# Linear attention into a two-layer MLP on one core: the first batch's preparation dealt out anew between GpSimd, ScalarE and VectorE, its first rows by head pairs, and two load gates moved

## The chip, the cores and the metric

The kernel runs on one core of one Trainium2 chip. The metric is device time in microseconds (us) of one execution; lower is better. The core has five engines that work through their own instruction streams: TensorE (PE; its weight loads are shown as PEld), VectorE (DVE), ScalarE (ACT), GpSimd (POOL) and SyncE (SP), which here only issues DMAs. GpSimd issues DMAs too. Engines wait for each other by semaphores.

## The reference

The computation is a linear attention, whose output is the input of a two-layer MLP with a leaky ReLU:

```
q, k, v: (8 batches, 8 heads, 576 rows, 64)   float32, 0.1 * randn
q_s = exp(q - max over the 64);       q_s /= sum over the 64
k_s = exp(k - max over the 576 rows); k_s /= sum over the 576 rows
kv  = k_s^T v      (64 x 64 for each batch and head)
a   = q_s kv       -> x: (4608 tokens, 512)
h   = x @ w_in     (512 x 2048)
g   = max(0.01 h, h)
out = g @ w_out    (2048 x 512), float32
```

## The kernel before, in words

*Layout.* A batch's q, k or v is one tile of 128 partitions x 4 head slots x 9 rows x 64. A partition holds 9 rows of a head, so 64 partitions are a head and a slot holds two heads, one on each half of the partitions. The name `gg` in the code counts pairs of slots (0 and 1), `hh` the half of the partitions. Column block g = 2 * hh + gg of x is 128 wide; there are four of them, and layer 1 takes them in the order 0, 2, 1, 3 (L451). So blocks 0 and 2 come from pair 0, blocks 1 and 3 from pair 1.

*Tiles of the MLP.* The 4608 tokens are nine tiles of 512. Layer 1 of a tile is 16 units (one per 128 columns of w_in), each followed by the leaky ReLU on ScalarE (`leaky`, L461); layer 2 accumulates over the same 16 blocks of w_out. Tile 0 is cut in two halves of 256 tokens for layer 1, so it has 32 units in pairs and then 16 steps of layer 2. The attention of the later batches is hung between these units: `at(t, u, ...)` (L484) puts functions behind unit u of tile t and `run` calls them, so the order of every engine's instructions is written out by hand; no scheduler moves them. Each engine works strictly in that order.

*Batch 0* has nothing to hide behind: its preparation is written out from L509 to L558. Its q is taken in three parts: rows 0 to 3 (`RA`, enough for the first 256 tokens), rows 4 and 5 (`R1`) and rows 6 to 8 (`R2`). The steps: `q_first` (L228) takes the maxima of q on VectorE and 16 small exps on ScalarE; `k_tree` (L149) takes k's maxima over the 9 rows on VectorE, `k_max_pe`, `k_all_dve` and `k_all_pe` carry them over the partitions with TensorE, `k_sub_ps` (L352) subtracts them on VectorE, `k_exp` (L202) is on ScalarE; `v_cast` (L209) turns v into bf16 for TensorE, on ScalarE for batch 0; `kv_pair` (L360) makes kv of one pair of slots, `kd_rec` and `kd_one` scale it into `kd`; `q_transpose` and `q_keep` turn the normalised q; `attend` (L408) multiplies it with kd and copies the result to xT. `wake` (L322) issues matmuls on a tile of zeros that nothing reads, which keep TensorE busy.

*Queues and gates.* SP issues, in this order, q's rows 0 to 3, the two halves of k, the two halves of v, q's other rows; then a tiny hold (`hold_sync`, L504: a copy of 256 bytes out of w_in, which makes SP wait for that piece of w_in), and behind it k, q and v of batch 1; then a hold on w_out and batch 2. GpSimd issues w_in in two halves of four loads (`load_w_in`, L129; half 0 is columns 0 to 1023, and of each half the first two loads are the column blocks 0 and 2, the last two the blocks 1 and 3), and w_out in five pieces. Ahead of each group stands a copy of one 4-byte element (a dummy, L510, L535, L565) that waits for some load or value, so that the group is not issued earlier.

*PSUM.* Six banks are shared by all short-lived products (`psB_pool`), two hold layer 2's sums. A matmul into a bank waits until the bank's last reader is done.

Tile 0's first four pairs of units take blocks 0 and 2 of all four first, and then, behind the attend of blocks 1 and 3, the rest:

```
for j in range(0, 8, 2):
    ...
    for i in range(2):
        layer1(j + i, ph[:, i], 0, 256, slice(0, 2), i == 0)
    ...
attend(0, [1, 3], 0, 256, nc.scalar)
```

Of the kernel before, what the change touches and what calls it, by code (L numbers as in the profile page):

```python
# [8 lines left out]
FP32 = mybir.dt.float32  # L9
# [11 lines left out]
R = 9  # L21
# [4 lines left out]
def kernel(  # L26
# [60 lines left out]
    R1, R2 = slice(4, 6), slice(6, R)  # L87
# [140 lines left out]
    def q_first(b, rs):  # L228

        n = rs.stop - rs.start  # L230
        nmax = small_pool.tile([P, HL, n], FP32, name="nmax")
        qsum = small_pool.tile([P, n, HL], FP32, name="qsum")
        for hs in (slice(0, 2), slice(2, 4)):
# [3 lines left out]
            for h in range(hs.start, hs.stop):  # L237
                for r in range(n):
                    nc.scalar.activation(
                        out=st[b]["qe"][:, rs.start + r, h],  # L240
                        in_=st[b]["q"][:, h, rs.start + r],
                        func=AF.Exp,
                        bias=nmax[:, h, r : r + 1],
                        accum_out=qsum[:, r, h : h + 1],
                    )
        st[b]["qsum"] = qsum

    def q_first_rec(b, rs):
        n = rs.stop - rs.start
        st[b]["qrec", rs.start] = qrec = small_pool.tile([P, n, HL], FP32, name="qrec")  # L250
        nc.vector.reciprocal(out=qrec, in_=st[b]["qsum"])
# [70 lines left out]
    def wake(n):  # L322
        for i in range(n):
            nc.tensor.matmul(  # L324
                wake_ps, lhsT=zero[:, 0:P], rhs=zero, start=(i == 0), stop=(i == n - 1)
            )
# [183 lines left out]
    nc.gpsimd.tensor_copy(out=gate[:, 0:1], in_=st[0]["k"][:, HL - 1, R - 1, D - 1 : D])  # L510
# [3 lines left out]
    q_first(0, RA)  # L514
    k_tree(0, H0)
# [6 lines left out]
    k_tree(0, H1, slice(1, 4))  # L522
    k_max_pe(0, 1)
# [5 lines left out]
    wake(2)  # L529
    k_sub_ps(0, 0, HB)  # L530
    k_exp(0, slice(1, 2))
    v_cast(nc.scalar, 0, 0)
    v_cast(nc.scalar, 0, 1)
    k_sub_ps(0, 1)
    nc.gpsimd.tensor_copy(out=gate[:, 0:1], in_=st[0]["k"][:, HL - 1, R - 1, D - 1 : D])  # L535
    load_w_in(1)
    k_exp(0, H1)
    q_first_rec(0, RA)
    q_norm(0, RA)
    kv_pair(0, 0)  # L540
    wake(4)
    q_transpose(0, 0, 4)
    kv_pair(0, 1)
    for hh in range(2):
        kd_rec(0, 0, hh)
        kd_one(nc.vector, 0, 0, hh)
    q_keep(nc.scalar, 0, 0, 4, slice(0, 4, 2))
    q_keep(nc.vector, 0, 0, 4, slice(1, 4, 2))
    attend(0, [0, 2], 0, 256, nc.scalar)
    wake(3)  # L550
    kd_rec(0, 1, 0)
    kd_rec(0, 1, 1)
    kd_one(nc.vector, 0, 1, 0)
    kd_one(nc.vector, 0, 1, 1)
    q_max(0, R1)
    q_sub(nc.gpsimd, 0, R1)
    q_max(0, R2)
# [169 lines left out]
```

## Time and profile before

| | |
|---|---|
| Time, median of 3 runs | 294.86 us (294.04 to 294.93) |
| Profiled execution | 294.82 us |
| Its span, first to last instruction | 293.0 us |
| TensorE (PE) busy | 282.1 us, 96% |
| PE weight loads | 139.9 us, 48% |
| VectorE (DVE) busy | 145.6 us, 50% |
| ScalarE (ACT) busy | 150.7 us, 51% |
| GpSimd (POOL) busy | 85.4 us, 29% |
| Chain that ended last | PE 85%, DVE 6%, POOL 2%, ACT 2% |
| DMA | 45.76 MB, mean 156 GB/s |

Times inside the execution are counted from the start of the span. The profiled execution is 1.8 us longer than its span; what lies outside is the same for any version of the program, so differences are taken inside the span. A row of a timeline gives the start, the duration, the engine, the line, the output tile and the inputs; in brackets stand the idle time before it and what ended that.

### The profile page before, as it was taken

What the parts mean: (1) busy time and instruction counts of PE and PEld (TensorE: products, weight loads), DVE (VectorE), ACT (ScalarE), POOL (GpSimd) and SP (SyncE); (2) the same over time, 40 slices, a digit from 0 to 9 for tenths busy, and PEclk for the clock granted to TensorE, in tenths of its full rate; (3) what the DMA queues carried; (4) which work ended last, traced back from release to release, by engine and by line L of the source; (5) the groups of instructions that cost most, each with busy time, mean ns of one, the idle gap of its engine ahead of it and who ended that gap; (6) DMA issues with size and microseconds to landing.
All of it is one profiled execution on the core that took longest, in us unless ns stands there. A gap on an engine that the chain in (4) does not pass through costs nothing.

```text
span 293.0 us, 4282 instructions
## 1 busy us (share of the span) xinstructions
PE 282.1 (96%) x1661; PEld 139.9 (48%) x1661; DVE 145.6 (50%) x240; ACT 150.7 (51%) x272; POOL 85.4 (29%) x61
## 2 busy tenths in 40 slices
PE   8698999999999999999999999999999999999995
PEld 2266845444544455454445544544455444444443
DVE  3946958696592597189367455735440200110011
ACT  4937684678058605951695338532854066007500
POOL 4645190008019307802930292029300000000000
PEclk9989999999999999999999999999999999999999
DMA  7999999496639553774399138933141310131032
GB/s 257 312 216 391 243 181 401 112 287 258 114 76 310 211 116 90 272 266 89 71 309 292 36 72 282 281 74 72 38 81 38 72 36 1 38 72 36 0 72 74
DMA packets 36580, 45.76 MB, mean 156 GB/s; under 512 B 15952, under 2 KB 19280, under 8 KB 36560
## 3 DMA queue, kind: packets, MB, share of 16 engines
q1 hardware_dynamic: 33120, 41.16, 47.9%
q0 software_dynamic: 3280, 4.20, 8.2%
q8 instruction: 13, 0.21, 0.3%
q10 hardware_dynamic: 160, 0.13, 0.1%
q14 instruction: 7, 0.06, 0.1%
HBM read 36.70 MB, written 9.44 MB: 157 GB/s over the span
## 4 chain that ended last, share of the span: by engine, by line
PE 85%; DVE 6%; POOL 2%; ACT 2%; issue 1%; POOLq 0%
PE pout L473 39%; PE ph L452 39%; PE pkv L295 2%; PE po L440 2%; DVE qe L280 1%; DVE qsum L273 1%; POOL k_raw L195 1%; DVE t L162 1%; PE pout L324 1%; PE psum_qt L389 1%; POOL q_raw L256 1%; PE po L412 1%; ACT xT L422 1%; PE pkv L365 1%; ACT qe L264 1%
## 5 line engine op out<-in xcount | busy, mean ns | idle before, releaser
L473 PE MATMUL pout<-w_out_sb,gj 128*128 128x512 bf16 (+2 forms) x592 | 130.4, 373 | 0.0
L452 PE MATMUL ph<-xT,w_in_sb 128*128 128x512 bf16 (+1 forms) x640 | 127.5, 358 | 1.6 <-ACT xT L422 1.6
L461 ACT ACTIVATE gj<-ph 128x512 bf16<-128x512 f32 x144 | 82.3, 604 | 58.1 <-PE ph L452 57.5
L452 PEld LDWEIGHTS <-w_in_sb 128*128 128x128 bf16 x640 | 62.1, 98 | 63.6 <-issue 2.9
L473 PEld LDWEIGHTS <-gj 128*128 128x128 bf16 x592 | 57.0, 98 | 61.8
L467 DVE COPY out_sb<-pout 128x512 f32<-128x512 f32 (+1 forms) x34 | 22.7, 675 | 90.3 <-PE pout L473 84.7
L195 POOL TENSOR_TENSOR k_raw<-k_raw,kall 128x2304 f32<-128x2304 f32 (+1 forms) x6 | 29.1, 4845 | 85.6 <-DVE kall L187 56.9
L256 POOL TENSOR_TENSOR q_raw<-q_raw,qmax 128x2304 f32<-128x2304 f32 (+4 forms) x11 | 31.1, 2836 | 25.8 <-DVE qmax L226 25.8
L273 DVE TENSOR_REDUCE qsum<-qe 128x36 f32<-128x2304 bf16 (+4 forms) x11 | 19.8, 1799 | 37.5 <-ACT qe L264 37.5
L446 ACT CAST xT<-po 128x320 bf16<-128x320 f32 (+1 forms) x48 | 16.8, 402 | 41.2 <-PE po L440 41.2
L203 ACT ACTIVATE ke<-k_raw 128x2304 bf16<-128x2304 f32 (+2 forms) x11 | 17.5, 1595 | 8.9 <-POOL k_raw L195 8.5
L280 DVE TENSOR_TENSOR qe<-qe,qrec 128x2304 bf16<-128x2304 bf16 (+4 forms) x12 | 21.7, 1807 | 0.4
L226 DVE TENSOR_REDUCE qmax<-q_raw 128x36 f32<-128x2304 f32 (+4 forms) x11 | 19.4, 1789 | 0.0
L264 ACT ACTIVATE qe<-q_raw 128x2304 bf16<-128x2304 f32 (+4 forms) x11 | 16.9, 1536 | 0.8 <-POOL q_raw L256 0.8
L215 POOL CAST vb<-v_raw 128x1152 bf16<-128x1152 f32 x12 | 13.4, 1148 | 0.0
L324 PE MATMUL pout<-zero 128*128 128x512 bf16 x27 | 10.5, 536 | 1.3 <-POOL zero L101 1.3
L162 DVE TENSOR_TENSOR t<-k_raw 128x1024 f32<-128x1024 f32 (+1 forms) x10 | 10.1, 1011 | 0.5 <-DMA k_raw<-in_k_dram 0.2
L467 ACT COPY out_sb<-pout 128x512 f32<-128x512 f32 (+1 forms) x3 | 1.7, 550 | 16.2 <-PE pout L473 16.2
L162 DVE TENSOR_TENSOR t<-t 128x256 f32<-128x256 f32 (+2 forms) x20 | 9.6, 478 | 0.6
L440 PE MATMUL po<-qX,kd 128*128 128x320 bf16 (+1 forms) x48 | 9.8, 286 | 0.0
L295 PEld LDWEIGHTS <-ke 64*128 64x128 bf16 x252 | 7.2, 93 | 3.0 <-ACT gj L461 1.7
L313 DVE TENSOR_TENSOR kd<-pkv,krec 64x128 bf16<-64x128 f32 x28 | 8.1, 289 | 0.7
(55 smaller groups left out, 104.2 us busy)
## 6 DMA issues: line engine op xcount, KB each, us to landing
out_dram<-out_sb SPq DMA_DIRECT2D x70, 128.0 KB, 2.4
q_raw<-in_q_dram SPq DMA_DIRECT2D x7, 1152.0 KB, 8.4
v_raw<-in_v_dram SPq DMA_DIRECT2D x7, 1152.0 KB, 11.0
k_raw<-in_k_dram SPq DMA_DIRECT2D x6, 1152.0 KB, 6.0
k_raw<-in_k_dram SPq DMA_DIRECT2D x4, 576.0 KB, 5.8
w_in_sb<-in_moe_w_in_dram POOLq DMA_DIRECT2D x8, 256.0 KB, 6.8
w_out_sb<-in_moe_w_out_dram POOLq DMA_DIRECT2D x3, 512.0 KB, 12.3
v_raw<-in_v_dram SPq DMA_DIRECT2D x2, 576.0 KB, 7.4
```

The lines of the kernel that those rows point to most:

```text
L162: nc.vector.tensor_tensor(out=o, in0=i0, in1=i1, op=ALU.max)
L195: eng.tensor_tensor(out=ks, in0=ks, in1=st[b]["kall"][:, hs].unsqueeze(2).to_broadcast([P, n, R, D]), op=ALU.subtract,)
L203: nc.scalar.activation(out=st[b]["ke"][:, :, hs].rearrange("p r h d -> p h r d"), in_=st[b]["k"][:, hs], func=AF.Exp,)
L226: nc.vector.tensor_reduce(out=m, in_=st[b]["q"][:, :, rs], axis=AX.X, op=ALU.max)
L256: eng.tensor_tensor(out=qs, in0=qs, in1=st[b]["qmax", rs.start].unsqueeze(3).to_broadcast([P, HL, n, D]), op=ALU.subtract,)
L264: nc.scalar.activation(out=st[b]["qe"][:, rs].rearrange("p r h d -> p h r d"), in_=st[b]["q"][:, :, rs], func=AF.Exp,)
L273: nc.vector.reduce_sum(out=qsum, in_=st[b]["qe"][:, rs], axis=AX.X)
L280: nc.vector.tensor_tensor(out=qes, in0=qes, in1=st[b]["qrec", rs.start].unsqueeze(3).to_broadcast([P, n, HL, D]), op=ALU.mult,)
L452: nc.tensor.matmul(ph, lhsT=w_in_sb[:, cb, j * P : (j + 1) * P], rhs=xT[:, cb, c0 : c0 + n], start=(i == 0 and first), stop=(i == NB - 1 a ...
L461: nc.scalar.activation(out=o, in_=ph, func=AF.Prelu, alpha=LEAKY_SLOPE)
L467: copy(out=out_sb, in_=pout)
L473: nc.tensor.matmul(pout, lhsT=g_sb[j // 2][:, j % 2, tsub * P : (tsub + 1) * P], rhs=w_out_sb[:, j, os], start=(j == 0), stop=(j == NF - 1),)
```

## The change

The diff works on batch 0 and on tile 0's units, and moves some functions of batch 1 between units.

- *Casts of v* for batch 0 go from ScalarE to GpSimd (`v_cast(nc.gpsimd, 0, 0)` and `(nc.gpsimd, 0, 1)`), and GpSimd normalises q's first rows, pair 0 between the casts, pair 1 behind them (`q_first_norm`), where VectorE did all of it in one instruction. `q_first` keeps its sums by pairs and `q_first_rec` is called once for each.
- *By pairs.* Rows 0 to 3 of q are transposed (`q_turn_first`) and kept (`q_keep_first`) pair by pair, and x's blocks 0 and 2 are attended one at a time, before the second pair's kv. The first units of layer 1 take block 0, then block 2 (`begin`), with blocks 1 and 3 attended between (`x1`), and finish with blocks 1 and 3 (`end`). The units of columns 8 to 15 are begun in the same way.
- *Late rows* are three pieces now: rows 4 and 5, 6 and 7, 8. Their subtractions on GpSimd stand ahead of w_out's loads, whose issue moves into a function called behind the first unit. Their exps, sums and normalisations, transposes and attends get other units.
- *Dummies.* The first one waits for the first half of k instead of the second; the one ahead of w_in's second half is replaced by one that waits for k's maxima and stands ahead of the casts, and w_in's second half follows the second normalisation. SP's first hold reads block 1 of w_in's second half (its third load) instead of block 0 (its first).
- *Warm-ups.* Four small float32 matmuls on the maxima of q stand behind the first 14 (`wake_on`); of the others, four zeros before q's transposes become three behind them, and two become three behind k's second maxima.
- *Batch 1.* v's casts stand together ahead of its exps, one group of q's transposes and the eight attends move by some units, and every second copy of these goes to VectorE. The stores of tile 0 are written behind the last step's functions instead of ahead of them.

```
-    R1, R2 = slice(4, 6), slice(6, R)
+    R1, R2, R3 = slice(4, 6), slice(6, 8), slice(8, R)
...
+        st[b]["nmax"] = nmax = small_pool.tile([P, HL, n], FP32, name="nmax")
+        for gg in range(2):
+            hs = slice(2 * gg, 2 * gg + 2)
+            st[b]["qsum", gg] = qsum = small_pool.tile([P, n, 2], FP32, name="qsum2")
...
+    def q_first_rec(b, gg):
+        st[b]["qrec2", gg] = qrec = small_pool.tile([P, RA.stop, 2], FP32, name="qrec2")
+        nc.vector.reciprocal(out=qrec, in_=st[b]["qsum", gg])
+
+    def q_first_norm(eng, b, gg):
+        qes = st[b]["qe"][:, RA, 2 * gg : 2 * gg + 2]
+        eng.tensor_tensor(
+            out=qes,
+            in0=qes,
+            in1=st[b]["qrec2", gg].unsqueeze(3).to_broadcast([P, RA.stop, 2, D]),
+            op=ALU.mult,
+        )
+
+    def q_turn_first(b, gg):
+        n = RA.stop
+        ps = psB_pool.tile([P, 2, n, L], BF16, name="psum_q2", tag=BANK_TAG)
+        for r in range(n):
+            nc.tensor.matmul(
+                ps[:, :, r],
+                lhsT=st[b]["qe"][:, r, 2 * gg : 2 * gg + 2].rearrange("p h d -> p (h d)"),
+                rhs=ident,
+                is_transpose=True,
...
+    def q_keep_first(eng, b, gg):
+        o, i = st[b]["qT"][:, gg::2, RA], st[b]["ps2", gg]
...
+    def wake_on(a, n):
+        for i in range(n):
+            nc.tensor.matmul(
+                wake_ps[0:RA.stop, 0:P], lhsT=a[:, HL - 1], rhs=identf, start=True, stop=True
+            )
...
     wake(14)
-    nc.gpsimd.tensor_copy(out=gate[:, 0:1], in_=st[0]["k"][:, HL - 1, R - 1, D - 1 : D])
+    nc.gpsimd.tensor_copy(out=gate[:, 0:1], in_=st[0]["k"][:, 1, R - 1, D - 1 : D])
     load_w_in(0)
     k_begin(0)
     q_begin(0)
     q_first(0, RA)
+    wake_on(st[0]["nmax"], 4)
     k_tree(0, H0)
...
     k_tree(0, H1, slice(1, 4))
+    nc.gpsimd.tensor_copy(out=gate[:, 0:1], in_=st[0]["kmax"][:, HL - 1, D - 1 : D])
+    v_cast(nc.gpsimd, 0, 0)
...
-    wake(2)
+    wake(3)
+    q_first_rec(0, 0)
+    q_first_norm(nc.gpsimd, 0, 0)
+    v_cast(nc.gpsimd, 0, 1)
     k_sub_ps(0, 0, HB)
     k_exp(0, slice(1, 2))
-    v_cast(nc.scalar, 0, 0)
-    v_cast(nc.scalar, 0, 1)
+    q_first_rec(0, 1)
+    q_first_norm(nc.gpsimd, 0, 1)
+    load_w_in(1)
     k_sub_ps(0, 1)
-    nc.gpsimd.tensor_copy(out=gate[:, 0:1], in_=st[0]["k"][:, HL - 1, R - 1, D - 1 : D])
-    load_w_in(1)
     k_exp(0, H1)
-    q_first_rec(0, RA)
-    q_norm(0, RA)
     kv_pair(0, 0)
-    wake(4)
-    q_transpose(0, 0, 4)
-    kv_pair(0, 1)
...
+    q_turn_first(0, 0)
     wake(3)
+    kd_rec(0, 0, 0)
+    kd_one(nc.vector, 0, 0, 0)
+    q_keep_first(nc.vector, 0, 0)
+    kd_rec(0, 0, 1)
+    kd_one(nc.vector, 0, 0, 1)
     q_max(0, R1)
     q_sub(nc.gpsimd, 0, R1)
+    attend(0, [0], 0, 256, nc.scalar)
+    kv_pair(0, 1)
+    attend(0, [2], 0, 256, nc.scalar)
+    q_turn_first(0, 1)
+    q_keep_first(nc.scalar, 0, 1)
+    for hh in range(2):
+        kd_rec(0, 1, hh)
+        kd_one(nc.vector, 0, 1, hh)
     q_max(0, R2)
     q_sub(nc.gpsimd, 0, R2)
 
-    hold_sync(0, w_in_sb[0:1, 0, F - 128 : F])
+    hold_sync(0, w_in_sb[0:1, 1, F - 128 : F])
...
+    def behind_first_units():
+        nc.gpsimd.tensor_copy(out=gate[:, 0:1], in_=st[1]["k"][:, 0, 0, 0:1])
+        for j0, j1 in ((0, 2), (2, 4), (4, 8), (8, 12), (12, 16)):
+            load_w_out(slice(j0, j1))
+        hold_sync(1, w_out_sb[0:1, 11, 0:128])
+        load_all(2)
...
+    at(0, 0, behind_first_units, lambda: q_rest(R1))
+    at(0, 3, lambda: q_rest(R2))
+    at(0, 13, lambda: attend(0, [0, 2], 256, 256, nc.scalar))
+    at(0, 13, lambda: attend(0, [1, 3], 256, 256, nc.vector))
+    at(0, 13, lambda: q_rest(R3))
+    at(0, 17, lambda: q_transpose(0, 8, 1), lambda: q_keep(nc.scalar, 0, 8, 1))
+    at(0, 21, lambda: attend(0, [0, 1, 2, 3], 512, 64, nc.scalar))
...
-    at(0, 29, lambda: k_exp(1, H1))
-    at(0, 31, lambda: v_cast(nc.scalar, 1, 0), lambda: k_exp(1, H0))
+    at(0, 31, lambda: v_cast(nc.scalar, 1, 0), lambda: v_cast(nc.scalar, 1, 1))
     at(0, 33, lambda: q_exp(1, RA), lambda: q_sum(1, RA), lambda: q_norm(1, RA))
-    at(0, 33, lambda: v_cast(nc.scalar, 1, 1), lambda: q_exp(1, RB), lambda: q_sum(1, RB))
+    at(0, 33, lambda: k_exp(1, H1), lambda: k_exp(1, H0), lambda: q_exp(1, RB))
...
-        at(0, 43, lambda r0=r0, n=n: q_transpose(1, r0, n), lambda r0=r0, n=n: q_keep(nc.scalar, 1, r0, n))
+        at(0, 44, lambda r0=r0, n=n: q_transpose(1, r0, n), lambda r0=r0, n=n: q_keep(nc.scalar, 1, r0, n))
     for i in range(8):
-        at(0, (45, 45, 46, 46, 46, 47, 47, 47)[i], lambda i=i: attend(1, [GS[i // 2]], 288 * (i % 2), 288, nc.scalar))
+        at(0, 46 + i // 4, lambda i=i: attend(1, [GS[i // 2]], 288 * (i % 2), 288, (nc.scalar, nc.vector)[i % 2]))
...
+    def begin(js, parts):
+        phs = [psB_pool.tile([P, 2, 256], FP32, name="ph", tag=BANK_TAG) for _ in js]
+        for i, between in parts:
+            for j, ph in zip(js, phs):
+                for h in range(2):
+                    layer1(j + h, ph[:, h], 0, 256, slice(i, i + 1), h == 0, False)
+            for fn in between:
+                fn()
+        return phs
+
+    def end(j, ph, half, part, first):
+        for h in range(2):
+            layer1(j + h, ph[:, h], 256 * half, 256, part, first and h == 0, h == 1)
+            if h == 1:
+                leaky(g_sb[j // 2][:, :, 256 * half : 256 * half + 256], ph)
+            run(0, 16 * half + j + h)
+
+    def x1():
+        attend(0, [1], 0, 256, nc.scalar)
+        attend(0, [3], 0, 256, nc.vector)
+        q_max(0, R3)
+        q_sub(nc.gpsimd, 0, R3)
+
+    t1 = (lambda: q_transpose(0, 4, 2), lambda: q_keep(nc.scalar, 0, 4, 2))
+    t2 = (lambda: q_transpose(0, 6, 2), lambda: q_keep(nc.vector, 0, 6, 2))
+    for j0, parts in ((0, ((0, (x1,)), (1, ()))), (8, ((0, t2), (1, ())))):
+        js = range(j0, j0 + 8, 2)
+        if j0:
+            for fn in t1:
+                fn()
+        for j, ph in zip(js, begin(js, parts)):
+            end(j, ph, 0, slice(2, 4), False)
+    for j in range(0, NF, 2):
+        end(j, psB_pool.tile([P, 2, 256], FP32, name="ph", tag=BANK_TAG), 1, slice(0, 4), True)
...
-        if j == NF - 1:
-            for tsub in range(NTS):
-                store(tsub * P, pout[tsub])
         run(0, 32 + j)
+    for tsub in range(NTS):
+        store(tsub * P, pout[tsub])
```

More of the change, by code (lines that the diff above doesn't have):

```diff
@@ L644 @@
     g_sb = g_tiles()
[L645 to L660 removed]
+    def begin(js, parts):
[8 more added lines that the diff above has]
+    def end(j, ph, half, part, first):
+        for h in range(2):
+            layer1(j + h, ph[:, h], 256 * half, 256, part, first and h == 0, h == 1)
[18 more added lines that the diff above has]
+        end(j, psB_pool.tile([P, 2, 256], FP32, name="ph", tag=BANK_TAG), 1, slice(0, 4), True)
     pout = [psO_pool.tile([P, O], FP32, name="pout") for _ in range(2)]
```

68 lines of the change are left out of this document (17 added, 51 removed).

## The prediction

> **What bounds the kernel now.** I read the page first (TensorE's share, the 40 slices), then the timeline of the first 45 us, the landing of single transfers, and the busy time by stretches of 2 us.
>
> ```profile
> span 293.0 us, 4282 instructions
> PE 282.1 (96%) x1661; PEld 139.9 (48%) x1661; DVE 145.6 (50%) x240; ACT 150.7 (51%) x272; POOL 85.4 (29%) x61
> DMA  7999999496639553774399138933141310131032
> ```
>
> TensorE is busy for 96% and its steady stages (from 55 us on) have nearly no gaps; the change touches only what comes before. The DMA row stands at 9 in the six slices after the first (7.3 to 51 us), so the start is a race of two streams: engine work, and 15 MB of loads.
>
> ```profile
> 12.03 2.19 ACT L213 CAST vb<-v_raw 128x1152 bf16<-128x1152 f32 x2
> 13.21 0.85 PE L365 MATMUL pkv<-vb,ke 64*128 64x129 bf16 x18 [1.45 <-ACT vb L213]
> 13.99 1.89 PE L324 MATMUL pout<-zero 128*128 128x512 bf16 x4
> 18.50 1.91 PE L452 MATMUL ph<-xT,w_in_sb 128*128 128x256 bf16 x16
> 36.03 3.74 POOL L195 TENSOR_TENSOR k_raw<-k_raw,kall 128x1152 f32<-128x1152 f32 x1 [6.52 <-DVE kall L187]
> 37.11 8.15 PE L473 MATMUL pout<-w_out_sb,gj 128*128 128x512 bf16 x37
> ```
>
> Columns: start, duration, engine, line, tiles, and in brackets the idle time before and who ended it. TensorE waits 1.45 us for v's first cast on ScalarE; layer 1 of tile 0 starts at 18.50 and ends at 37.0 though its 128 matmuls at 0.107 us (8 in 1.03 in the rows from 30 us on), 12 attend matmuls and 10 late transposes are only 15.3 us of work: 3.2 us of it are waits. Layer 2 starts at 37.11.
>
> ```profile
> 18.79 0.63 SPq L505 DMA_DIRECT2D held<-w_in_sb  x1
> 19.46 1.08 SPq L79 DMA_DIRECT2D k_raw<-in_k_dram  x2
> ```
> ```profile
> w_in_sb<-in_moe_w_in_dram POOLq DMA_DIRECT2D x1, 256.0 KB, 7.3
> k_raw<-in_k_dram SPq DMA_DIRECT2D x1, 576.0 KB, 5.8
> w_out_sb<-in_moe_w_out_dram POOLq DMA_DIRECT2D x1, 512.0 KB, 10.5
> ```
>
> The last number is us from issue to landing, each of one transfer: the third of the four w_in loads of the second half (issued 14.03, so landed 21.3), the first load of batch 1 (19.46, 25.2) and w_out's third piece, rows 4 to 7 (27.25, 37.77). Read the same way, w_in's second half landed at 18.8, 20.0, 21.3 and 22.5, w_out's pieces at 33.2, 35.2, 37.8, 40.35 and 42.85: evenly spaced, one queue that is never empty.
>
> ```profile
> 12.00:14.00 2.00, 0.79 (x19) 0.59 (x19) 1.97 (x3) 2.00 (x3) 1.24 (x3) 0.90 1.12 208
> 14.00:16.00 2.00, 2.00 (x10) 0.90 (x9) 1.04 (x5) 1.28 (x2) 1.25 (x3) 0.50 1.12 209
> 38.00:40.00 2.00, 2.00 (x11) 0.94 (x10) 1.79 (x2) 2.00 (x4) 2.00 (x2) 1.00 1.25 205
> 40.00:42.00 2.00, 2.00 (x11) 0.90 (x10) 0.00 (x0) 1.39 (x2) 2.00 (x2) 1.00 0.71 115
> ```
>
> Busy us of PE, PEld, DVE, ACT, POOL, then granted clock, DMA share, GB/s. The clock is halved in 14 to 16; the DMA share falls under 1 only at 40 to 42, behind SP's second hold. Layer 2 needs w_out row 4 after 16 matmuls at 0.2157: 37.11 + 3.45 = 40.56, so that piece is 2.8 us early, the tightest of the five. This slack is what the change can spend.
>
> **The change part by part**, in times of the profiled execution (294.82 us; span 293.0; the median is 294.86).
>
> *v's casts go to GpSimd* (1.14 us each there and on ScalarE), with the two normalisations between. GpSimd: first dummy when k's first half lands (issued 1.26, landed 6.13; before it was the second half, 7.64), four w_in issues of 2.56 us, over at 9.3. The second dummy waits for kmax (9.87). Then cast 1.14, normalise 1.04 (nearest row: GpSimd's 512-element subtract at 19.22), cast, normalise: 10.1 to 14.5. A normalisation in bf16 is not in the trace; by the 3.74 us row (3.25 ns an element) it is at most 1.66, by the cast rows (1 ns) at least 0.5; 1.04 is the same shape.
>
> *VectorE* gets two reciprocals (0.2 each) ahead of k's subtractions, loses the 1.23 normalisation. k's second exp ends at 12.5 instead of 12.12, so the first kv pair runs at 12.5, not 13.21: 0.7 us won, v's cast (11.3) no longer in the way. *The 14 warm-ups get four small matmuls on nmax behind them:* k's transpose starts only at 8.1, and the zeros end at 7.2, so their 0.5 to 1.1 us (the kallp rows, four in 0.44, at either clock) cost 0 to 0.2; I take 0.
>
> *q and x by head pairs.* From the kv pair (13.2): reciprocal and kd 0.54, transposes and the keep (0.42) to 14.2, attend 0.28, ScalarE's copy 0.4. The other pair waits for the exp of k's last two heads (14.4): kv 0.7, attend, four transposes, then layer 1 at 15.3, against 18.50: 3.2 us earlier. 1.9 of this is the four zeros that ran at half clock.
>
> *Late q rows in three pieces.* GpSimd must issue w_in's second half (14.5 to 16.9) before it subtracts for R1 (1.04), so ScalarE's exp starts at 18.0 and VectorE's sum, reciprocal and normalise (0.69, 0.2, 0.69) put R1's transposes at 20.4, R2's at 22.1. TensorE finishes its first four units at 19.4 and waits there about 1 us, then 0.7 more; its units of columns 8 to 15 end their second half only when w_in's last load is in (22.5). From 23.1 on, 80 matmuls (8.6), attends and transposes (0.9) and the two waits for an xT copy that the trace has too (1.3 together) put the end of layer 1 at 33.9, against 37.0: 3.1 us earlier. R3's chain is covered by these units.
>
> *Queues.* w_in's second half is issued 1.6 us later (14.5). Before, its first load landed 1.25 us behind the last of the first half (17.52), so it stood in the queue. A lone load costs 2.1 to 2.7 us over its transfer (stores of 128 KB 2.4, the 0.2 KB hold 2.7): 14.5 + 2.6 + 1.25 = 18.4, under 18.8, hidden. The other end is the shortest landing that a GpSimd load shows, 5.8 us: 20.3, so 1.5 us late. I take 0, because those 5.8 us were spent behind q's last rows, which landed 1.05 us before it.
>
> SP's first hold now reads the third w_in load, not the first, with batch 1's four loads behind it. It is released at 21.3 instead of 18.78, and k goes out at 22.0: 2.55 us later. Before, k waited behind w_in's last load, so only part shows. Low end: 22.0 + 2.1 + 1.5 (576 KB) = 25.6, 0.4 late; high end the full 2.55. I take 1.2: the DMA engines finished w_in at about 21.7 to 22.2, and a load's first bytes come about 1.1 us after its issue (estimate: half of the 2.1 to 2.7), at 23.1, 0.9 to 1.5 later than they could have. SP's second hold is 0.6 us from piece to next issue in the trace and leaves a hole as well. Everything behind in the queue moves by these 1.2: q, v, w_out. GpSimd's dummy and w_out's five issues (3.7 us) start at 26.6 instead of 25.34; they are now behind R1 to R3's subtractions (done by 19.7), which cost nothing.
>
> *What is late next.* w_out's row 4 is there at 37.77 + 1.2 = 39.0, while TensorE, at 33.9 + 3.45, could use it at 37.4. So layer 2 passes row 4 at 39.0 and not 40.56: 1.56 us earlier, and 1.6 of the 3.1 us are lost in front of w_out. Rows 8 and 12 (41.55, 44.05) are asked for at 42.5 and 47.7 and are no bound. Batch 1 keeps up: its tree waits for k (26.4, 27.9) but starts 2.4 us before the 29.93 of the trace, v's casts on ScalarE wait for v (34.6 + 1.2), and q's second normalisation ends near 46.5, before the transposes moved to the unit after row 12 (48.5). Four of the last eight copies go to VectorE, the stores behind them: about 0.2 lost at the seam to tile 1 (last copy 0.45 behind the last attend, 0.65 of matmuls before its column is read, against 0.2 idle in the trace). Later tiles are untouched, with loads 1.2 later and over 3 us of room.
>
> Sum: 294.82 - 1.56 + 0.2 = 293.5.
>
> **A rule against the trace.** The 3.74 us of GpSimd's subtraction ran beside a VectorE subtraction of 1.36 with both inputs in SBUF; at 1.81 ns an element (the 4.18 us of the next two) it would be 2.09. The Trainium skill, "SBUF — State Buffer", section "Who interferes with whom", has it that a VectorE instruction with two SBUF inputs shuts out a GpSimd one that reads SBUF, and one with a single SBUF input does not. The trace agrees with the first half; no run here shows the second. By that rule the casts beside k's subtractions (one input in PSUM) keep their 1.14 and the sum stays 293.5; without it the third rival's 295.8 comes out.
>
> **The rivals.**
> 1. *The queue closes up.* If the hole behind SP's hold is 0.2 or less, w_out's row 4 comes at 38.0: 2.6 - 0.2 = 2.4 us won, 292.4. For it: the engine that lands last sets each landing and was late by up to 1.5 us (k's landing is 2.7 behind w_in's last, for 1.5 of transfer), so a pause lets it catch up. Against it: 1.8 us from release to first bytes.
> 2. *No change.* Both unknowns at their high side: a shift of 2.7 puts row 4 at 40.5; with the 0.2, 294.9. For it: no GpSimd load in the trace landed under 5.8 us.
> 3. *GpSimd blocked by VectorE (slower).* k's subtractions (0.75, 0.67, 1.35) lie in 9.9 to 13.2, beside the casts; if each shuts GpSimd out, w_in's second half goes out at 17.3, lands from 21.1, 2.3 late, and the shift is 3.5: row 4 at 41.3, 295.8. It decides from a shift of 2.8 on. Against it: those read PSUM.
> 4. *The clock falls again.* The 56% busy of 10 to 14 us were followed by half clock to 17. The waits before w_out leave about 65%; 26 to 30 us had 61% and kept it. If it falls, 3.4 us at half speed cost 1.7: 295.2.
>
> **How the numbers follow.** Forecast 0.47 (shift 0.4 to 1.9: 292.7 to 294.2), rival 1 0.18, rival 2 0.20, rival 3 0.10, rival 4 0.05. The three runs of before lie 0.3% apart (294.04 to 294.93), so 0.3% (0.9 us) is what can be told from no change: under 294.0 is faster. Rival 1 and nine tenths of the forecast: 0.60; rival 2, the rest of the forecast and a little of 4: 0.27; rivals 3 and 4: 0.13. The range, 292.3 to 295.2, leaves out rival 3 and some of 1.
>
> **What would show it.** Right: the first kv pair near 12.5, layer 1 from about 15.3 at full clock, waits of TensorE at 19.4 to 22, layer 1 over near 34, then waits that a w_out transfer ends, rows 4 to 7 landing near 39, a DMA dip at 22 to 23, tile 1 from about 53.2. Wrong: casts on GpSimd well over 1.2 us, w_in's second half landing after 19.5, a halved clock after 34, or w_out landing where it did.

## The result: slower, and the profile after

The changed kernel takes 295.81 us (median of 20 runs, 294.70 to 297.09), the kernel before 294.02 (20 runs, 293.85 to 296.74): a ratio of 1.0037, 95% interval 1.0021 to 1.0054. The ratio is smaller than that of the two medians (1.0061): 8 of the 20 executions before took 294.86 us or more. The profiled execution took 295.54 us. The forecast was 293.5.

The page of the changed kernel first: its span, the DMA row of the 40 slices and the chain that ended last.

```profile
span 293.8 us, 4273 instructions
...
DMA  7996998799448653964389138933141310131033
...
PE 84%; DMA 10%; POOL 2%; DVE 1%; issue 1%; SPq 0%; ACT 0%; POOLq 0%; ACTq 0%
```

Before, transfers had no share in the chain and VectorE had 6%; now transfers hold 10% of it. The part of it before layer 2 runs through the later issue and the moved hold (start, duration, what): w_in's third load from its issue, SP's hold on it, batch 1's k, GpSimd's issue of w_out, and the landing of w_out's rows 4 to 7, for which layer 2 waits.

```profile
15.78 7.50 DMA w_in_sb<-in_moe_w_in_dram
...
23.29 0.63 SPq L540
...
23.97 3.95 DMA k_raw<-in_k_dram
...
28.49 1.47 POOL w_out_sb L140 x2
29.96 11.72 DMA w_out_sb<-in_moe_w_out_dram
...
41.72 5.34 PE pout L508 x24
```

The row of 9s has a dent in the fourth slice (22 to 29 us). The timeline of TensorE and of SP's queue shows where (start, duration, engine, and in brackets the idle time before and who ended it):

```profile
12.46 0.68 PE L400 MATMUL pkv<-vb,ke 64*128 64x129 bf16 x18 [0.26 <-ACT ke L203]
...
15.28 1.08 PE L487 MATMUL ph<-xT,w_in_sb 128*128 128x256 bf16 x8
...
20.56 0.38 PE L424 MATMUL psum_qt<-ident,qe 128*128 128x128 bf16 x4 [0.97 <-DVE qe L309]
...
21.85 1.84 PE L487 MATMUL ph<-xT,w_in_sb 128*128 128x256 bf16 x8 [0.91 <-DMA w_in_sb<-in_moe_w_in_dram]
...
23.29 0.63 SPq L540 DMA_DIRECT2D held<-w_in_sb  x1
...
23.97 1.08 SPq L79 DMA_DIRECT2D k_raw<-in_k_dram  x2
...
37.67 3.61 PE L508 MATMUL pout<-w_out_sb,gj 128*128 128x512 bf16 x15 [1.42 <-DMA w_out_sb<-in_moe_w_out_dram]
...
41.72 5.34 PE L508 MATMUL pout<-w_out_sb,gj 128*128 128x512 bf16 x24 [0.43 <-DMA w_out_sb<-in_moe_w_out_dram]
```

Up to 20.56 all of it is as forecast: kv at 12.5, layer 1 from 15.3, R1's transposes at 20.4. Then come three waits for transfers. SP's hold opens at 23.29 (before: 18.79) and layer 2 passes row 4 of w_out at 41.72 (before: 40.56). The same stretch in windows of 2 us; the last three columns are the granted clock, the DMA share and GB/s:

```profile
16.00:18.00 2.00, 1.92 (x16) 1.29 (x15) 1.60 (x4) 0.49 (x2) 2.00 (x4) 1.00 1.08 189
18.00:20.00 2.00, 1.59 (x15) 1.17 (x12) 1.17 (x3) 1.90 (x4) 1.62 (x3) 1.00 1.07 178
20.00:22.00 2.00, 0.53 (x6) 0.37 (x7) 1.90 (x4) 1.67 (x4) 0.00 (x0) 0.98 1.07 166
22.00:24.00 2.00, 2.00 (x13) 1.57 (x12) 0.00 (x0) 0.00 (x0) 0.00 (x0) 0.50 0.49 90
24.00:26.00 2.00, 2.00 (x15) 1.55 (x13) 0.42 (x1) 0.00 (x0) 0.00 (x0) 0.67 0.27 52
```

The kernel before:

```profile
18.00:20.00 2.00, 1.97 (x17) 1.45 (x15) 1.99 (x4) 0.44 (x1) 0.78 (x1) 1.00 1.12 209
20.00:22.00 2.00, 1.33 (x13) 1.04 (x12) 0.00 (x0) 0.66 (x2) 1.69 (x2) 1.00 1.12 235
22.00:24.00 2.00, 2.00 (x20) 1.80 (x19) 0.44 (x1) 2.00 (x5) 0.00 (x0) 1.00 1.03 367
```

Two faults of the transfers stand here. From 16 to 22 the DMA engines are busy (1.07) but move 166 to 189 GB/s, where the kernel before had 209 and more: w_in's second half, issued at 14.55, lands at 19.41, 21.72, 23.28 and 24.52 (before: 18.77, 20.02, 21.32, 22.54). From 22 to 26 they are idle for (1.05 - 0.49) x 2 + (1.05 - 0.27) x 2 = 2.7 us: nothing but the last of w_in is in any queue, since SP stands at its hold until 23.29, issues k at 23.97, and k's first packet moves at 25.18. The single landings, read off the trace, for all versions (us; "SP" is the release of its first hold, "k" the first load of batch 1, "4-7" the landing of w_out's rows 4 to 7, "layer 2" its start, "tile 1" the start of that tile's layer 1). Each row shows one execution beside the median of all; that of "R1 to R3 on VectorE" took 297.13 us. The medians below the third row come from three later series, in which the kernel before had 294.54 (for the next four rows), 294.14 (the three behind those) and 294.05 (the last three); each ratio below is to the kernel before of its own series.

| version | w_in last | SP | k | 4-7 | layer 2 | tile 1 | median, us |
|---|---|---|---|---|---|---|---|
| before | 22.54 | 18.79 | 25.22 | 37.77 | 37.11 | 54.60 | 294.02 |
| before, another execution | 23.22 | 19.25 | 25.39 | 37.90 | 35.88 | 53.37 | (293.64) |
| after | 24.52 | 23.29 | 27.92 | 41.68 | waits to 37.67 | 55.58 | 295.81 |
| after, hold on first load | 24.76 | 19.10 | 26.22 | 39.43 | 35.50 | 53.67 | 293.94 |
| before, hold on third load | 23.19 | 21.90 | 27.3 | 40.84 | 36.38 | 54.45 | 294.51 |
| after, w_in issued earlier | 23.71 | 21.89 | 26.51 | 40.29 | 35.33 | 54.19 | 294.88 |
| both of these | 23.69 | 18.88 | 24.96 | 37.52 | 35.09 | 53.27 | 293.95 |
| R1 to R3 on VectorE | 25.88 | 24.64 | 29.57 | 43.28 | waits to 39.46 | 57.18 | 295.98 |
| the same, hold on first | 24.87 | 19.26 | 26.21 | 38.79 | 35.60 | 53.77 | 293.91 |
| second cast on ScalarE | 23.81 | 19.34 | 25.22 | 37.96 | 34.55 | 52.73 | 292.60 |
| the same, issue delayed | 24.22 | 19.86 | 25.67 | 38.57 | 34.96 | 53.13 | 293.35 |
| second cast on ScalarE, first dummy on k's first half | 23.81 | 18.85 | 25.04 | 37.61 | 34.55 | 52.72 | 292.67 |
| the same, pair 1 between units | 23.99 | 18.86 | 25.08 | 37.67 | 34.73 | 52.92 | 292.87 |

### The profile page after: what moved, and what is told of

It is laid out like the page before. It is cut to its first block, busy times and chain, and to the rows that moved or that the text cites. A ratio compares the mean times of both kernels' runs of the same rounds, so it can differ in the third digit from the quotient of the medians.

```text
span 293.8 us, 4273 instructions
## 1 busy us (share of the span) xinstructions
PE 280.8 (96%) x1639; PEld 140.1 (48%) x1666; DVE 146.5 (50%) x248; ACT 148.1 (50%) x270; POOL 90.3 (31%) x66
## 4 chain that ended last, share of the span: by engine, by line
PE 84%; DMA 10%; POOL 2%; DVE 1%; issue 1%; SPq 0%; ACT 0%; POOLq 0%; ACTq 0%
PE pout L508 41%; PE ph L487 37%; DMA w_out_sb<-in_moe_w_out_dram 4%; DMA k_raw<-in_k_dram 3%; PE pkv L324 3%; DMA w_in_sb<-in_moe_w_in_dram 3%; PE po L475 2%; DVE t L162 1%; POOL vb L215 1%; POOL qe L254 1%; POOL w_out_sb L140 0%; PE psum_qt L424 0%; POOL w_in_sb L133 0%; SPq L540 0%; PE po L447 0%
## 5 line engine op out<-in xcount | busy, mean ns | idle before, releaser
L487 PEld LDWEIGHTS <-w_in_sb 128*128 128x128 bf16 x640 | 62.8, 99 | 63.8 <-issue 2.6
L203 ACT ACTIVATE ke<-k_raw 128x2304 bf16<-128x2304 f32 (+2 forms) x11 | 17.4, 1594 | 10.8 <-POOL k_raw L195 8.6
L309 DVE TENSOR_TENSOR qe<-qe,qrec 128x2304 bf16<-128x2304 bf16 (+4 forms) x12 | 20.6, 1717 | 0.4
L215 POOL CAST vb<-v_raw 128x1152 bf16<-128x1152 f32 x14 | 15.7, 1149 | 0.0
L353 PE MATMUL pout<-zero 128*128 128x512 bf16 x23 | 7.7, 471 | 1.4 <-POOL zero L101 1.3
```

Source lines behind the costliest of these rows:

```text
L203: nc.scalar.activation(out=st[b]["ke"][:, :, hs].rearrange("p r h d -> p h r d"), in_=st[b]["k"][:, hs], func=AF.Exp,)
L215: eng.tensor_copy(out=o, in_=i)
L309: nc.vector.tensor_tensor(out=qes, in0=qes, in1=st[b]["qrec", rs.start].unsqueeze(3).to_broadcast([P, n, HL, D]), op=ALU.mult,)
L487: nc.tensor.matmul(ph, lhsT=w_in_sb[:, cb, j * P : (j + 1) * P], rhs=xT[:, cb, c0 : c0 + n], start=(i == 0 and first), stop=(i == NB - 1 a ...
```

## The experiments

My theory was that the loss sits in two places of the DMA queues that the change touched: (a) SP's hold, which reads w_in's third load and not its first, and (b) the later issue of w_in's second half. The rival was that the engines' new order costs the time, through GpSimd or the clock.

### The hold alone

```
-    hold_sync(0, w_in_sb[0:1, 1, F - 128 : F])
+    hold_sync(0, w_in_sb[0:1, 0, F - 128 : F])
```

On the changed kernel:

> The changed kernel with SP's first hold put back on the first load of w_in's second half. Theory A (the hold on the third load opens the hole in the DMA stream): in the changed kernel SP was released at 23.3 and the DMA share was 0.49 and 0.27 in 22 to 24 and 24 to 26 us; here SP is released near 19.4, batch 1's k stands in the queue behind w_in, the share stays at 1 there, k's first half lands near 26.5 instead of 27.9 and w_out's rows 4 to 7 near 39.3 instead of 41.7; about 1.8 us below the changed kernel, at or a little under the kernel before. Theory B (w_in's second half is issued too late, the hold adds little): the hole shrinks, but the whole is within 0.5 us of the changed kernel.

On the kernel before, the other way round (hold on the third load):

> The kernel before with only the hold moved to the third load of w_in's second half. Theory A: SP is released at 21.3 instead of 18.8, a hole of 1 to 1.5 us opens behind w_in, w_out's rows 4 to 7 land near 39.1 instead of 37.8, still ahead of their use at 40.6: the time stays within 0.3 us. Theory C (any lateness of batch 1's loads costs at once, through batch 1's preparation): 1 us or more slower.

The changed kernel with its hold on the first load: 293.94 us (12 runs), ratio to the kernel before 0.9984 (0.9961 to 1.0007). Its windows:

```profile
18.00:20.00 2.00, 1.69 (x16) 1.27 (x13) 1.08 (x3) 1.81 (x4) 1.72 (x3) 1.00 1.12 178
...
22.00:24.00 2.00, 1.59 (x17) 1.20 (x14) 0.49 (x2) 0.00 (x0) 0.00 (x0) 1.00 1.06 255
24.00:26.00 2.00, 1.11 (x11) 1.02 (x12) 0.00 (x0) 0.47 (x1) 0.00 (x0) 1.00 1.03 378
```

The hole is gone (1.06 and 1.03), and with it 1.0037 - 0.9984 = 0.53%, or 1.6 us: more than the whole loss, near the 1.8 of theory A, whose landings came too (26.22 and 39.43). The 178 GB/s between 18 and 20 stay, and TensorE now waits 1.31 us for w_in's last load.

The kernel before with the hold on the third load: 294.51 us, ratio 0.9998 (0.9973 to 1.0023). The hole appears here too:

```profile
22.00:24.00 2.00, 1.15 (x12) 0.82 (x10) 1.31 (x3) 2.00 (x5) 0.00 (x0) 1.00 0.39 36
24.00:26.00 2.00, 2.00 (x22) 1.67 (x19) 1.93 (x4) 1.38 (x3) 0.00 (x0) 1.00 0.69 166
```
```profile
38.44 1.89 PE L473 MATMUL pout<-w_out_sb,gj 128*128 128x512 bf16 x8 [0.17 <-DMA w_out_sb<-in_moe_w_out_dram]
...
40.88 5.34 PE L473 MATMUL pout<-w_out_sb,gj 128*128 128x512 bf16 x24 [0.55 <-DMA w_out_sb<-in_moe_w_out_dram]
```

The DMA engines are idle for (1.05 - 0.39) x 2 + (1.05 - 0.69) x 2 = 2.0 us, k lands at 27.30, and w_out's rows 4 to 7 at 40.84: 3 us later than in the two executions of the kernel before (37.77 and 37.90), where 39.1 was expected. That uses up w_out's slack and TensorE waits 0.72 us there, no more; between the two kernels' times no difference can be measured, to 0.25% on either side. (By single profiles it would look dearer: row 4 is passed at 40.88 here, at 39.33 and 40.56 in the two executions of the kernel before.) So the hold costs at most that where w_in lands on time (21.88, SP on at 21.90) and w_out has slack, and twice as much in the changed kernel, where w_in lands late and layer 2 could start sooner.

### The issue of w_in, alone and with the hold

```
     q_first_norm(nc.gpsimd, 0, 0)
+    load_w_in(1)
     v_cast(nc.gpsimd, 0, 1)
...
     q_first_norm(nc.gpsimd, 0, 1)
-    load_w_in(1)
```

> The changed kernel with w_in's second half issued between the first normalisation and the second cast on GpSimd, so at 12.6 instead of 14.5; the second pair's cast and normalisation come 2.4 us later. Theory B: w_in's second half lands as before the change (18.8 to 22.5 instead of 19.4 to 24.5), TensorE's wait at 21.9 and the half clock of 22 to 25 vanish, SP is released near 21.4, w_out's rows 4 to 7 land near 39.3; layer 1 starts near 17.5 instead of 15.3; the time is 1.5 us below the changed kernel. Theory A: most of the hole stays (1.5 of 2.6 us), and the gain is under 1 us.

With the hold on the first load as well:

> Both: w_in's second half issued at 12.6, and SP's hold on its first load. If the two delays of the DMA stream are the whole loss, w_out's rows 4 to 7 land near 37.8 as before the change, layer 1 ends near 34, row 4 is reached at 37.8 to 38, and the time is 2.4 us under the kernel before (near 291.7 on the median of 294.0). If the rearranged engine work has a price of its own, it shows here: less than 1 us under the kernel before, with w_out landing early and TensorE waiting for something else.

Issued at 12.76, the third load landed at 21.87 instead of 23.28, and SP went on at 21.89: 294.88 us, ratio 0.9991 (0.9968 to 1.0014). That is 0.46%, or 1.4 us, under the change, near theory B's 1.5; the wait at 21.9 and the half clock are gone, but w_in's last load landed at 23.71, not 22.5, and w_out's rows at 40.29, not 39.3. With both edits 293.95, ratio 0.9970 (0.9946 to 0.9994). Against the 1.0037 of the change the two edits gain 0.46% and 0.53% alone and 0.67% together: less than their sum, though with intervals of about 0.25% on each side of every ratio that alone proves nothing. The timeline of the version with both shows what a sum leaves out:

```profile
16.19 0.69 PE L400 MATMUL pkv<-vb,ke 64*128 64x129 bf16 x18 [1.72 <-POOL vb L215]
...
35.09 8.80 PE L508 MATMUL pout<-w_out_sb,gj 128*128 128x512 bf16 x40
...
48.86 0.72 PE L424 MATMUL psum_qt<-ident,qe 128*128 128x128 bf16 x10 [0.70 <-DVE kd L342]
```

Layer 2 runs 40 matmuls without a wait, so w_out is no longer the bound. But kv of the second pair waits 1.72 us for the cast that now stands behind the 2.44 us of issuing, and layer 1 starts at 17.43 instead of 15.3. So this case's issue on GpSimd is not free for what stands behind it. Of the expected gain of 2.4 us on the kernel before, 0.30%, or 0.9 us, came. Layer 2 began at 35.09 where about 34 was expected. The clock has a part as well: the six of the 12 executions with a mean granted clock of 0.994 took 294.44 to 294.99 us, the six at 0.999 and over 293.21 to 293.47.

### What makes w_in late: GpSimd's work behind the issue, or the issue itself

```
-    q_sub(nc.gpsimd, 0, R1)
+    q_sub(nc.vector, 0, R1)
```

(and the same for R2 and R3), with the hold of the change and with the hold on the first load:

> The change with the three subtractions of the late q rows on VectorE instead of GpSimd, nothing else; the issue of w_in's second half stays at 14.55. If the late issue itself makes the loads late: landings within 0.4 of the 19.4, 21.7, 23.3 and 24.5 of the change, SP released near 23.3, time 295.8 us as the change (294.9 to 296.2, since R1's rows are ready earlier). Rival: GpSimd's subtractions right behind the issue slow the loads: landings 18.9, 20.1, 21.4 and 22.6, SP released near 21.4, w_out's rows 4 to 7 near 39.8, about 294.3 us.

> The same with SP's first hold on the first load. If the late issue makes the loads late: w_in's second half at 19.1, 21.3, 23.4 and 24.8 as with the hold moved alone, and 293.9 us (293.4 to 294.3). Rival (GpSimd's subtractions slow the loads): 18.9, 20.1, 21.4 and 22.6, k at 25.2, w_out's rows 4 to 7 at 37.8, no wait for w_in, 292.9 us.

295.98 us, ratio 1.0055 (1.0028 to 1.0082), and 293.91, ratio 0.9978 (0.9959 to 0.9998): as the change and as the change with its hold moved. With GpSimd idle behind its issue (0.00 in the fifth column from 18 on) the transfers are no faster:

```profile
18.00:20.00 2.00, 1.62 (x16) 1.29 (x15) 1.97 (x5) 0.79 (x3) 0.00 (x0) 1.00 1.12 181
20.00:22.00 2.00, 1.08 (x11) 0.62 (x8) 1.90 (x5) 2.00 (x6) 0.00 (x0) 1.00 1.03 138
```

So GpSimd's subtractions are not the cause. The landings of the first of these two were later than either side expected (23.42, 24.63 and 25.88 for the last three loads): of the second load's 16 pieces most were in by 20.3, and the last came 3 us behind them. The second version met its expectation (19.25, 21.38, 23.18 and 24.87, and 293.91 us).

### A version with the issue early and the cast elsewhere

The hold is on the first load and the first dummy on k's second half, as in the kernel before; w_in's second half is issued behind GpSimd's first cast, the second cast is on ScalarE between k's exps, and pair 0 is normalised on VectorE:

```
     wake(3)
+    load_w_in(1)
     q_first_rec(0, 0)
-    q_first_norm(nc.gpsimd, 0, 0)
-    v_cast(nc.gpsimd, 0, 1)
     k_sub_ps(0, 0, HB)
     k_exp(0, slice(1, 2))
+    v_cast(nc.scalar, 0, 1)
+    q_first_norm(nc.vector, 0, 0)
     q_first_rec(0, 1)
     q_first_norm(nc.gpsimd, 0, 1)
-    load_w_in(1)
     k_sub_ps(0, 1)
```

> The change with SP's first hold on the first load again, w_in's second half issued right behind the first cast on GpSimd (about 11.6 instead of 14.55), the second cast on ScalarE between k's exps, pair 0's normalisation on VectorE, and the first dummy back on k's second half. If lateness of the issue and the hold are all that was lost: w_in's second half lands at 18.8, 20.0, 21.3 and 22.5, no hole in the DMA share between 20 and 26, w_out's rows 4 to 7 at 37.6, layer 1 from 15.7 (17.43 in the version with both edits, because its cast came behind the issue), layer 2 from about 34 with waits for w_out up to row 4: tile 1 about 1 us earlier than in the version with both edits, 292.5 us. Rival: batch 1's chain of VectorE and ScalarE (the 0.70 us wait for kd there) is the bound whatever layer 1 does: 293.3 us and a wait of over 1 us ahead of batch 1's kv or its transposes.

292.60 us (6 runs, 292.12 to 293.31), ratio 0.9941 (0.9919 to 0.9963): faster than both kernels. Windows and timeline:

```profile
18.00:20.00 2.00, 2.00 (x21) 1.78 (x19) 1.86 (x5) 1.48 (x4) 1.44 (x2) 1.00 1.12 207
20.00:22.00 2.00, 1.16 (x12) 0.73 (x10) 1.46 (x4) 2.00 (x5) 0.00 (x0) 1.00 1.11 211
```
```profile
21.49 1.03 PE L487 MATMUL ph<-xT,w_in_sb 128*128 128x256 bf16 x8 [0.80 <-DMA w_in_sb<-in_moe_w_in_dram]
...
23.94 1.47 PE L487 MATMUL ph<-xT,w_in_sb 128*128 128x256 bf16 x12 [0.32 <-DMA w_in_sb<-in_moe_w_in_dram]
...
34.55 8.80 PE L508 MATMUL pout<-w_out_sb,gj 128*128 128x512 bf16 x40
...
48.32 0.72 PE L424 MATMUL psum_qt<-ident,qe 128*128 128x128 bf16 x10 [0.70 <-DVE kd L342]
```

Issued at 12.18, w_in moves at 207 to 211 GB/s again, there is no hole, and w_out is never waited for. Of the 1.35 us between this median and that of the version with both edits (another series), about 0.6 is the clock: all six executions here were at 1.0, and the six of the other at 0.999 and over have a median of 293.3. The time came as expected (292.5) with landings that did not: 19.33, 21.36, 22.26 and 23.81, up to 1.4 us later than the 18.8, 20.0, 21.3 and 22.5 that it was worked out from, so it was in part luck. The rival (batch 1's chain is the bound whatever comes before, 293.3) is refuted as to the time; its wait for kd is there, with 0.70 us as before.

Then one thing is put back into this version: the issue is delayed, by a fill of a spare tile on GpSimd.

```
+    spare = const_pool.tile([P, 1536], FP32)
...
-    load_w_in(1)
     q_first_rec(0, 0)
...
     q_first_norm(nc.gpsimd, 0, 1)
+    nc.gpsimd.memset(spare, 0.0)
+    load_w_in(1)
```

> The fast version with the second cast on ScalarE, in which one thing is put back: w_in's second half is issued at about 14.7 instead of 12.18, behind pair 1's normalisation and a fill of 1536 elements on GpSimd (some 1.5 us, work that does nothing else). If the time of the issue is what spoils the transfers: 178 to 190 GB/s instead of 207 to 211 between 18 and 22, last landing near 24.8 instead of 23.8, 293.6 us (293.2 to 294.2) instead of 292.6. Rival, that the engines' other work of 18 to 22 spoils them (it differs between the change and this version): 205 GB/s or more, landings within 0.3 of 19.3, 21.4, 22.3 and 23.8, 292.7 us.

293.35 us (10 runs, 293.00 to 294.65), ratio 0.9969 (0.9946 to 0.9991). Without the delay it was 0.9941 (0.9919 to 0.9963) in another series, and the intervals overlap; the two versions with an early issue that ran beside this one (next section) had 292.67 and 292.87, 0.5 to 0.7 us less. The issue began at 15.22:

```profile
18.00:20.00 2.00, 2.00 (x20) 1.68 (x18) 0.88 (x2) 1.23 (x3) 2.00 (x3) 1.00 1.07 188
20.00:22.00 2.00, 0.92 (x12) 0.74 (x11) 1.86 (x6) 2.00 (x5) 0.30 (x1) 1.00 1.03 147
```

The low rate is back: 188 and 147, where the same order on the other engines had 207 and 211. The last load came at 24.22, earlier than the 24.8 expected and 0.4 later than without the delay. A load lands with the last of its 16 pieces, and that hides most of the effect: the eighth piece of the last load came at 23.66 here and at 22.45 without the delay, 1.2 us apart, but without the delay the slowest pieces straggled further. So the time of the issue alone brings the low rate.

### What bounds the version now

The first dummy as the change has it (k's first half):

```
-    nc.gpsimd.tensor_copy(out=gate[:, 0:1], in_=st[0]["k"][:, HL - 1, R - 1, D - 1 : D])
+    nc.gpsimd.tensor_copy(out=gate[:, 0:1], in_=st[0]["k"][:, 1, R - 1, D - 1 : D])
```

> The fast version with the first dummy as the change has it, on k's first half: w_in's first half is issued at about 7.1 instead of 8.44, q's late rows land near 14.8. If the earlier issue brings w_in forward: the first half's last load near 17.6 instead of 18.1, the second half's near 18.9, 20.3, 21.5 and 23.7, the wait of 0.80 us at 21.49 gone, 292.2 us. Rival: the loads share the same DMA engines, so w_in gains nothing in the end and q's late rows lose 2 us: a wait ahead of R1's transposes in place of it, 292.6 us or more.

And with pair 0's normalisation on GpSimd again, and pair 1's transposes behind the first eight matmuls of layer 1:

```
+    q_first_norm(nc.gpsimd, 0, 0)
     load_w_in(1)
...
-    q_first_norm(nc.vector, 0, 0)
...
-    q_turn_first(0, 1)
-    q_keep_first(nc.scalar, 0, 1)
...
+    def x0():
+        q_turn_first(0, 1)
+        q_keep_first(nc.scalar, 0, 1)
...
-    for j0, parts in ((0, ((0, (x1,)), (1, ()))),
+    for j0, parts in ((0, ((0, (x0,)), (1, (x1,)))),
```

> The version before this with pair 0's normalisation on GpSimd again, ahead of the issue (12.5 instead of 12.2), and pair 1's transposes of q put behind the first eight matmuls of layer 1. Layer 1 from 15.3 instead of 16.38, as in the change. If layer 1's end is set by w_in's last load (23.7) and not by its start: layer 2 from 34.2 to 34.6 as before and 292.2 to 292.6 us. Rival, its start sets it: layer 2 from 33.5 with a wait for w_out's rows 2 to 7, 291.8 us.

292.67 us, ratio 0.9936 (0.9912 to 0.9960), and 292.87, ratio 0.9938 (0.9913 to 0.9963): both as the version before them. The earlier first dummy brought the last load of w_in's first half forward by 0.5 us (17.59), that of the second not at all (23.81 in both), and TensorE still waited 0.99 us at 21.17: the expected 292.2 did not come, nor did the wait ahead of R1's transposes that the rival named. In the second, layer 1 starts 1 us earlier and nothing comes of it:

```profile
15.38 1.04 PE L487 MATMUL ph<-xT,w_in_sb 128*128 128x256 bf16 x8
...
21.27 1.03 PE L487 MATMUL ph<-xT,w_in_sb 128*128 128x256 bf16 x8 [0.51 <-DMA w_in_sb<-in_moe_w_in_dram]
...
24.13 1.47 PE L487 MATMUL ph<-xT,w_in_sb 128*128 128x256 bf16 x12 [0.72 <-DMA w_in_sb<-in_moe_w_in_dram]
...
34.73 8.80 PE L508 MATMUL pout<-w_out_sb,gj 128*128 128x512 bf16 x40
```

From the last load's wait to layer 2 it is 34.73 - 24.13 = 10.60 us, and as much in the version before (34.55 - 23.94 = 10.61) and in the change with its hold on the first load (35.50 - 24.89 = 10.61). Where layer 1 in the change's order has to wait for w_in's last load, its end is that load plus 10.6, wherever layer 1 began. In the two versions in which it began late (17.67 and 17.43) it did not wait, and layer 2 came 11.6 and 11.4 us behind the load.

### The kernel before, a second time

> The kernel before, unchanged, for a second profile. If the half clock of 13.6 to 17.0 belongs to one execution and not to the kernel (the clock's windows run free of the kernel's start): other instants of half clock or none, layer 1 from about 17.5 where the four zeros ran at full clock, and a span up to 1 us shorter. If it belongs to the kernel: half clock again from about 13.6 and layer 1 at 18.5.

One execution, 293.64 us, with no half clock in its first 18 us:

```profile
14.05 1.04 PE L324 MATMUL pout<-zero 128*128 128x512 bf16 x4
...
17.27 1.91 PE L452 MATMUL ph<-xT,w_in_sb 128*128 128x256 bf16 x16
...
23.36 1.69 PE L452 MATMUL ph<-xT,w_in_sb 128*128 128x256 bf16 x14 [1.17 <-DMA w_in_sb<-in_moe_w_in_dram]
...
35.88 8.80 PE L473 MATMUL pout<-w_out_sb,gj 128*128 128x512 bf16 x40
```

The four zeros took 1.04 us, not 1.89, layer 1 began at 17.27, not 18.50, layer 2 at 35.88, not 37.11, and the whole was 1.2 us shorter. The half clock belongs to the execution, not to the kernel. Its end of layer 1, too, hangs on w_in's last load (a wait of 1.17), with 12.5 us behind it where the change's order has 10.6.

## Why the prediction was wrong, step by step

*The engine side was right.* GpSimd's casts and normalisations take 1.15 and 1.05 (forecast 1.14 and 1.04). They run beside VectorE's subtractions without being held up, VectorE and GpSimd of the changed kernel:

```profile
10.01 0.75 DVE L391 TENSOR_TENSOR k_raw<-k_raw,kallp 128x576 f32<-128x576 f32 x1
...
10.35 1.15 POOL L215 CAST vb<-v_raw 128x1152 bf16<-128x1152 f32 x1
...
11.72 1.30 DVE L391 TENSOR_TENSOR k_raw<-k_raw,kallp 128x1152 f32<-128x1152 f32 x1
...
12.46 1.15 POOL L215 CAST vb<-v_raw 128x1152 bf16<-128x1152 f32 x1
```

Rival 3 falls with this as a mechanism, though its time, 295.8, is what came out. The second half of the rule that was weighed there (the Trainium skill, "SBUF — State Buffer", "Who interferes with whom": a VectorE instruction with one SBUF input leaves GpSimd its port) agrees with these 1.15 us.

*The step that failed is "Queues".* Both of its terms did.
- "18.4, under 18.8, hidden" took w_in's lateness as 0. The first load landed at 19.41. What the step left out is that all four loads also move more slowly when they are issued this late: 166 to 189 GB/s instead of 209. The third load was 1.96 us late, the fourth 1.98 (1.5 and 1.3 against the second execution of the kernel before). The delayed issue shows that the time of the issue is enough for the low rate. In w_out's rows 4 to 7, which the sum goes by, this term is 41.68 - 40.29 = 1.4 us, by the version with the earlier issue.
- The hold on the third load was taken at 1.2 with 2.55 as its high end, and everything behind k was moved by k's own shift. Alone, in the kernel before, it cost w_out's rows 3 us (40.84) while k came only 2.1 later (27.30 against 25.22); why w_out lost 1 us more than k was not tested. In the changed kernel the lateness of the third load came on top: 2.55 by the choice of the load and 1.96 by its lateness, so k went out 23.97 - 19.46 = 4.5 us later, landed 2.7 later, and w_out's rows 4 to 7 landed 3.9 later, not 1.2.

The two terms work through one gate, since SP goes on when the third load lands. So mending either one alone brings the change back to even with the kernel before (0.9984, 0.9961 to 1.0007, with the hold moved; 0.9991, 0.9968 to 1.0014, with the earlier issue). In w_out's rows the moved hold is worth 41.68 - 39.43 = 2.25 us, the earlier issue 1.39, and both 41.68 - 37.52 = 4.16, in one execution each.

By the sum's own terms: layer 2 passes row 4 at 41.72, + 1.16 instead of - 1.56. The seam to tile 1 and the rest are shorter by 0.3 to 0.4 (from row 4 to the end of the span 293.8 - 41.72 = 252.1, before 293.0 - 40.56 = 252.4), where 0.2 had been added. 294.82 + 1.16 - 0.35 = 295.6, against 295.54 measured.

*A slip in the rivals.* Rival 2 calls itself both unknowns at their high side, but its shift of 2.7 is 1.5 + 1.2, with the hold at the value taken and not at its high end. Both at the high side are 1.5 + 2.55 = 4.05: row 4 at 41.8. That is nearly what was measured, and by the sum it gives 296.3 us. With its upper end at 295.2, the range left that case out, and ended 0.6 us too low.

*Too much was made of the profiled execution.* "3.2 us earlier" for layer 1 held against 18.50; against the second execution of the kernel before it is 17.27 - 15.28 = 2.0. There row 4 is passed at 35.88 + 3.45 = 39.33, so that a forecast of 39.0 would have gained 0.3 us and not 1.56. Most of the forecast gain was one stretch of half clock at a place where it cost 1.2 us; the median of 294.02 lies 0.8 us below that execution, too.

*What bounds layer 1* was seen ("end their second half only when w_in's last load is in (22.5)") and its 10.8 us of work behind that are 10.6. The start of layer 1 was still treated as the gain, and w_in's lateness as harmless.

*Rival 4* (half clock after 34 us) didn't happen. The clock fell at 22 instead, after a window with TensorE busy for 0.53 of 2 us; it can have cost little, since TensorE then waited 1.42 and 0.43 us for w_out anyway. Nor is the clock the cause of the loss: the 14 of the changed kernel's 20 executions with a mean granted clock of 0.998 or over took 294.70 to 296.73 us (median 295.34), the 11 such executions of the kernel before in the later series 293.50 to 294.17.

## What to carry to other kernels

A gate in a queue passes the lateness of what it reads on to all that stands behind it: before moving one, work out the DMA engines' idle time between the gated piece's landing and the next bytes, and add its high end to the high end of the piece's own lateness. Where a stage has to wait for its last load, an earlier start of the stage is worth nothing; keep the issue early and give the engine's other work away, as the version at 292.6 us does. And look at a second execution before taking a gap of the profile as gain.

## What the runs showed of the hardware that was not expected

- Loads that GpSimd issued at 14.6 to 15.2 us moved 178 to 188 GB/s between 18 and 20 in all five versions that did so, though the DMA engines were busy (1.05 to 1.12); issued at 11.5 to 13.4, the same loads moved 202 to 214 in all eight executions. The packets of 2 KB between 18 and 20 took 0.17 us for the most part everywhere, but in the five versions 11 to 32 of their 166 to 184 took over 0.2 (up to 0.75 in the changed kernel), in the eight at most 3 of about 200. Neither GpSimd's later work nor the order on the other engines makes the difference; what does, between issue and transfer, stays open.
- A program load of 16 KB goes through the same DMA engines and holds one of them for 0.95 us. The queues of the changed kernel between 18 and 20 us (packets, MB, share):

```profile
q0 software_dynamic: 190, 0.34, 103.7%
q8 instruction: 1, 0.02, 3.0%
```

It came at 18.95, in w_in's second load; in the kernel before at 21.87, behind most of w_in. In the two last versions, where it came at 18.66 and 18.83, the second load's last piece was 1.2 and 1.3 us behind the eleventh of its 16, and in each of the last three loads a single piece came 0.91 to 1.04 us behind the fifteenth. That fits one engine being held, and no run tested it. It is not the cause of the low rate: in the version with the delayed issue it came at 17.06, ahead of these loads, and the rate was low; in the two last versions it came among them, and the rate was 214.
- Half clock comes in pieces of one length: in the changed kernel (1 - 0.98) + (1 - 0.50) + (1 - 0.67) over windows of 2 us make 0.85 x 2 / 0.5 = 3.4 us, and the kernel before had 13.6 to 17.0. The Trainium skill, "TensorE: Matmul & The Clock Gate", section "What's actually happening", gives a window of 3.4 us that runs free of the kernel's start; the two executions of the kernel before, one with such a piece at 13.6 and one with none up to 290 us, agree. In the 3.41 us ahead of the three drops seen inside a kernel TensorE was busy for 1.65 (before, at 13.6), 1.53 (after, at 21.9) and 0.93 us (R1 to R3 on VectorE, at 23.9); 1.51 of 3.40 us at 4.6 in the kernel before with its hold on the third load was followed by the full clock, so the busy share alone doesn't settle it. Of the kernel before, 30 of the 35 executions of the first later series had a mean granted clock of 0.983 to 0.994, where one such piece is 3.4 x 0.5 / 293 = 0.006; those at 0.988 and under, two pieces or more, took 295.2 us and over. All 40 executions of the versions with R1 to R3 on VectorE and the hold on the first load, and of the four versions with the second cast on ScalarE, were at 0.998 to 1.0; why no piece fell there was not looked into.
